# Opening products issued between the arms of a switch, tokens rounded to 16, scatters without order

## The chip, the cores and the metric

One core of a Trainium2 chip runs the whole program. The metric is device time in microseconds. Each kernel is run several times and the median is given; one execution is taken by the hardware profiler, and all rows and start times come from that one.

## The reference

Two stages. First, attention in chunks: 4 batches, 8 heads, 768 positions of 64 numbers; each chunk of 32 queries sees 8 memory keys, its own chunk, 16 keys to the left and 8 to the right. The outputs of all heads make a row x of 512 numbers for each of the 3072 tokens. Second, a mixture of 8 experts that drops no token:

```python
logits = x @ w_gate
expert_idx = np.argmax(logits, axis=1)
# gate_w: the softmax of the chosen expert
h = np.maximum(x_sorted[lo:hi] @ w1[e], 0.0)     # 512 -> 1024
y_sorted[lo:hi] = h @ w2[e]                       # 1024 -> 512
return gate_w[:, None] * y
```

All is fp32. How many tokens an expert has depends on the data. On the inputs of the reference the experts 0 to 7 get 529, 195, 426, 381, 565, 320, 162 and 494 tokens.

## The kernel before

**Attention and sorting** take the first 180 us or so. Finished rows of x are scattered by GpSimd into a DRAM area with one region for each expert. The first 256 tokens of expert 0 are worked on early, with plain matmuls (L1224, L1240). Meanwhile `count_up` counts the tokens of the experts, divides them into steps of STEP = 32 (rounded up) and writes `cases`, one number for each expert, and `good`, which says that the ordinary program's assumptions hold.

**The experts** come one after the other. Since the number of tokens is known only at run time, the program holds one copy of the body (an arm) for each possible number of steps: `tc.Switch(index[e], CASES)` with 33 arms. Each of the five engines loads the 8 numbers into registers (`loads`), and jumps on its own into the arm: in the trace these are COMPARE_BRANCH rows of line 1287, one for leaving an arm and one for entering the next.

**A body** (`expert`) of n tokens splits them into two halves of hf = n/2 columns, and computes both layers in a scheme of Strassen's kind: seven products of quarter matrices in the place of eight, and sums of quarters on VectorE. The first layer has 7 products for each of 2 column pairs, each of 4 matmuls; `product(i, bank, ...)` (L1081 is its matmul) writes one of six PSUM banks, taken in turn. The order on the engines is written out by hand (`manual_schedule`). A body opens with products 1 and 2 of both pairs into banks 0 to 3. ACT copies product 1 (L1107), VectorE adds product 2 (L1108). Then TensorE transposes two groups of the previous expert's result (`put_back`: `turn_y`, a scaling on ACT, and a scatter to `out` by GpSimd, L1021), goes on with product 6, transposes the other two groups, and so on. In the second half of the first layer it also transposes the next expert's tokens into `xT` (`turn_x`), and in `between` VectorE makes their sums and those of the next weights. The second layer has seven products of 8 matmuls, the last of them product 3 into bank 5, which `result` adds after the Switch (L1164).

More than 512 tokens are worked on in two bodies, one after the other, in one arm (expert 4); the argument `new` of `first_layer` is true in the first of them.

**Queues.** SyncE fetches the weights: four pieces of 512 KB for each layer, each behind the last reader of its buffer. GpSimd gathers the tokens of expert e + 2 in body e and scatters the results of expert e - 1. Since all scatters write the same tensor `out`, each of them waits until the one before has landed. After the last expert four more put-backs follow, then all engines load `good` (L1261) and jump over the general program, which runs when `good` is 0 (L1262).

Each fp32 matmul stands in the trace as two MATMUL rows with two LDWEIGHTS rows.

Of the kernel before, what the change touches and what calls it, by code (L numbers as in the profile page):

```python
# [70 lines left out]
XC = 1024  # L71
DX = 528
SKIP = 4096
STEP = 32
CASES = XC // STEP + 1
CAP = 512
HALF = CAP // 2
# [10 lines left out]
def parts(n):  # L88

    n1 = n if n <= CAP else STEP * -(-n // (2 * STEP))  # L90
    return [w for w in (n1, n - n1) if w]
# [419 lines left out]
def ordinary(ctx, tc, q, k, v, mem_k, mem_v, moe_w_gate, moe_w1, moe_w2, out, good):  # L511
# [503 lines left out]
    def gated(py, gate):  # L1015
        y = mpool.tile([128, DM], F32, name="y", bufs=4)
        nc.scalar.activation(y, py, AF.Copy, scale=gate)  # L1017
        return y

    def store(y, token):  # L1020
        nc.gpsimd.indirect_dma_start(  # L1021
            out=out,
            out_offset=bass.IndirectOffsetOnAxis(ap=token.bitcast(I32), axis=0),
            in_=y,
            in_offset=None,
            bounds_check=N - 1,
            oob_is_err=False,
        )

    def put_back(yT, tg, g):  # L1030

# [44 lines left out]
    def product(i, bank, w, a, q0):  # L1076

        hf, k = a[i].shape[2], a[i].shape[1]
        for q in range(2):
            for c in range(k):  # L1080
                mm(  # L1081
                    bank[:, q, 0:hf],
                    lhsT=w[i][:, c, 128 * (q0 + q) : 128 * (q0 + q) + 128],
                    rhs=a[i][:, c],
                    start=c == 0,
                    stop=c == k - 1,
                )
        return bank[:, :, 0:hf]

    def sums_of_x():  # L1090
        a = halves(xT, KX, HALF)
        sums(a, xS, slice(0, KX // 2))
        sum4(a, xS, slice(0, KX // 2))

    def first_layer(e, hf, backs, turns, new):

        a = halves(xT, KX, hf)
        w, a = weights(e, 0), streams(a, xS[:, :, :, 0:hf])
        hh, s = halves(h, KH, hf), hS[:, :, :, 0:hf]
        relu = lambda o: nc.scalar.activation(o, o, AF.Relu)  # L1100
        T = lambda i: tmp[:, i, :, 0:hf]
        C = lambda p: slice(2 * p, 2 * p + 2)
        to = lambda i, j, p: hh[i][j][:, C(p)]
        turn_of = iter(range(14))
        P = lambda i, p: product(i, banks[next(turn_of) % 6], w, a, 2 * p)
        for p in range(2):
            nc.scalar.copy(T(p), P(1, p))  # L1107
            i = add(to(0, 0, p), T(p), P(2, p), op=OP.add)  # L1108
            if p == 0 and new and e + 1 < E:
                for n in range(4):  # L1110
                    fetch_w(e + 1, 0, n, after=i)
            relu(to(0, 0, p))
        for f in backs[:2]:
            f()
        for p in range(2):
            add(T(p), T(p), P(6, p), op=OP.add)
        for f in backs[2:]:
            f()
        for p in range(2):
            add(T(2 + p), T(p), P(7, p), op=OP.add)  # L1120
        if new:
            sum_weights(e, 1, (5, 6))
        for p in range(2):
            p5 = P(5, p)
            add(to(1, 1, p), T(2 + p), p5, op=OP.add)  # L1125
            relu(to(1, 1, p))
            add(T(p), T(p), p5, op=OP.add)
        if new:
            sum_weights(e, 1, (4,))
        for p in range(2):  # L1130
            add(to(1, 0, p), T(2 + p), P(4, p), op=OP.add)
            relu(to(1, 0, p))
        for f in turns[:1]:
            f()
        for p in range(2):
            sums(hh, s, C(p))
            p3 = P(3, p)
            for f in turns[1:2] if p == 0 else turns[2:]:
                f()
            add(to(0, 1, p), T(p), p3, op=OP.add)  # L1140
            relu(to(0, 1, p))
        for p in range(2):
            sum4(hh, s, C(p))
        if new:
            sum_weights(e, 1, (7,))

    def second_layer(e, hf, yT, between):
        w, a = weights(e, 1), streams(halves(h, KH, hf), hS[:, :, :, 0:hf])
        p1, u2, u3 = (tmp[:, i, :, 0:hf] for i in (0, 4, 5))
        P = lambda i, b: product(i, banks[b], w, a, 0)  # L1150
        nc.scalar.copy(p1, P(1, 2))
        between()
        p4, p5 = P(4, 3), P(5, 4)
        add(u2, p1, P(6, 0), op=OP.add)
        add(u3, u2, P(7, 1), op=OP.add)
        add(yT[:, 2:4, 1, 0:hf], u3, p5, op=OP.add)
        add(u2, u2, p5, op=OP.add)
        add(yT[:, 0:2, 1, 0:hf], u3, p4, op=OP.add)
        add(yT[:, 0:2, 0, 0:hf], p1, P(2, 2), op=OP.add)
        P(3, 5)  # L1160

    def result(yT):
# [3 lines left out]
    def expert(e, n):  # L1166


        ps = parts(n)
        both = lambda f, *x: [lambda g=g: f(*x, g) for g in range(4)]  # L1170
        backs = both(put_back, yTs[(e - 1) % 2], tgs[(e - 1) % 2]) if e else []
        yT = yTs[e % 2]
        x = xes[e % 2]
        if len(ps) == 2:
            fetch_x(xe2, e, 1)
        for k, w in enumerate(ps or [0]):
            last = k + 1 >= len(ps)
            tg = tgs[e % 2 if last else 2]
            nc.vector.tensor_copy(tg, x[:, :, DM : DM + 2])
            if k == 0 and e + 2 < E:  # L1180
                fetch_x(x, e + 2, 0)
            x = xes[(e + 1) % 2] if last else xe2
            turns = both(turn_x, x) if not last or e + 1 < E else []
            if w:
                first_layer(e, w // 2, backs, turns, k == 0)
            else:
                for f in backs + turns:
                    f()
                if e + 1 < E:
                    for i in range(4):  # L1190
                        fetch_w(e + 1, 0, i)
            if last and e + 1 < E:
                for i in range(4):
                    fetch_w(e + 1, 1, i)

            def between():
                if turns:
                    sums_of_x()
                if last and e + 1 < E:
                    sum_weights(e + 1, 0)  # L1200

            if w:
                second_layer(e, w // 2, yT, between)
            else:
                between()
            if not last:
                result(yT)
                backs = both(put_back, yT, tg)

    def loads(engines, c, n):  # L1210
        return {eng.engine: eng.value_load(cases[0:1, c : c + 1], min_val=0, max_val=n - 1) for eng in engines}

    with tc.manual_schedule():
        choose(last)
        label(last)

        w1 = ws[0][0].rearrange("p (k n) -> p k n", n=F)
        w2 = ws[0][1].rearrange("p (k n) -> p k n", n=DM)
        for g in range(2):
            turn_x(xe2, g)  # L1220
        for f in range(KH):
            ph = banks[f % 4][:, 0]
            for c in range(KX):
                mm(ph, lhsT=w1[:, c, 128 * f : 128 * f + 128], rhs=xT[:, c, 0], start=c == 0, stop=c == KX - 1)  # L1224
            nc.scalar.activation(h[:, f, 0], ph, AF.Relu)
            if f == 1:
                rank(last, banks[4].rearrange("p a b -> p (a b)"))()
                count_up(banks[5])
                scatter(sent, NB)
        for t in [xes[1]] + yTs:  # L1230
            nc.vector.memset(t, 0.0)
        engines = (nc.tensor, nc.scalar, nc.vector, nc.gpsimd, nc.sync)
        index = [loads(engines, e, CASES) for e in range(E)]
        fetch_x(xes[0], 0, 0)
        fetch_x(xes[1], 1, 0)
        sum_weights(0, 0)
        for g in range(2):
            py = banks[4 + g].rearrange("p a b -> p (a b)")
            for f in range(KH):
                mm(py, lhsT=h[:, f, 0, 128 * g : 128 * g + 128], rhs=w2[:, f], start=f == 0, stop=f == KH - 1)  # L1240
            if g == 0:
                for g2 in range(4):
                    turn_x(xes[0], g2)
                sums_of_x()
            y = gated(py, xe2[:, g, DM + 1 : DM + 2])
            store(y, xe2[:, g, DM : DM + 1])
        for e in range(E):
            for a in tc.Switch(index[e], CASES):  # L1248
                expert(e, STEP * a)
            result(yTs[e % 2])  # L1250
        for g in range(4):
            put_back(yTs[(E - 1) % 2], tgs[(E - 1) % 2], g)


@with_exitstack
def kernel(ctx, tc, *args):
    nc = tc.nc
    gpool = ctx.enter_context(tc.tile_pool(name="gpool", bufs=1))
    good = gpool.tile([1, 1], I32, name="good")
    ordinary(tc, *args, good)  # L1260
    rv = nc.values_load(good[0:1, 0:1], min_val=0, max_val=1)  # L1261
    with tc.If(rv == 0):  # L1262
        general(tc, *args)

# [27 lines left out]
```

## Time and profile before

| | us |
|---|---|
| median of 6 runs | 607.2 (604.97 to 610.85) |
| profiled execution, its own time | 609.69 |
| its span, first to last instruction | 607.9 |
| TensorE busy in the span | 527.9 (87%) |
| mean granted clock of TensorE | 0.932 |
| experts' part, first opening to last product | 207.9 to 575.6 |
| idle before the openings of the bodies | 28.6 |

The widths hf seen in the trace are 144 (expert 0), 112, 224, 192, 144 twice (expert 4), 160, 96 and 256.

How to read it: a group's line has the source line, engine, operation, output and inputs, shapes and count, then the busy time and the mean of one in ns, then the idle time of the engine just before the group's instructions and what ended it. "issue" stands for a wait in which the profile shows nothing that was waited for. In timeline rows the first two numbers are start and duration. PEclk is the granted share of TensorE's clock in 40 slices of the span, in tenths.

### The profile page before, as it was taken

How to read it: one execution, taken by the hardware profiler on the slowest of the kernel's cores; microseconds unless marked ns; L12 is line 12 of the kernel's file. 1: busy time of each engine (PE TensorE's matmuls, PEld its weight loads, DVE VectorE, ACT ScalarE, POOL GpSimd, SP SyncE). 2: the span in 40 equal slices, each digit the busy share in tenths (PEclk: the TensorE clock that was granted, in tenths of full speed). 3: DMA queues.
4: the chain of work that ended last, by engine and by line, in shares of the span. 5: the costliest groups of instructions: out<-in, count | busy, mean ns of one | idle time of the engine just before them, and what ended most of it. 6: DMA issues, size and time to landing. Idle time of an engine off the chain costs nothing. (4 is left out here: it accounts for less than half of the span.)

```text
span 607.9 us, 10606 instructions
## 1 busy us (share of the span) xinstructions
PE 527.9 (87%) x3850; PEld 502.9 (83%) x3850; DVE 324.3 (53%) x757; ACT 176.2 (29%) x414; POOL 132.3 (22%) x174
## 2 busy tenths in 40 slices
PE   4999999999998998986998997999979799699900
PEld 3999899999976697986997997999879699588800
DVE  4556556565447286491782592655719639156300
ACT  3566365655311230221310320414023022122010
POOL 3500211412346320412200313301031011020020
PEclk9999899999869999997998998999979989799965
DMA  9999999997223190722520822503246063000010
GB/s 174 187 176 185 231 177 229 225 208 163 61 83 99 63 334 13 278 97 91 188 76 8 280 104 58 192 9 101 87 161 225 13 225 105 6 23 2 3 69 3
DMA packets 81658, 76.17 MB, mean 125 GB/s; under 512 B 39852, under 2 KB 64556, under 8 KB 81456
## 3 DMA queue, kind: packets, MB, share of 16 engines
q1 hardware_dynamic: 72368, 54.54, 38.2%
q0 software_dynamic: 8128, 19.29, 9.8%
q14 instruction: 147, 1.20, 0.7%
q8 instruction: 55, 0.90, 0.7%
q10 hardware_dynamic: 960, 0.24, 0.2%
HBM read 65.04 MB, written 16.45 MB: 134 GB/s over the span
## 5 line engine op out<-in xcount | busy, mean ns | idle before, releaser
L1081 PE MATMUL b<-xT,w 128*128 128x144 f32 (+6 forms) x288 | 58.4, 377 | 28.6 <-issue 25.6
L1081 PEld LDWEIGHTS b<-xT,w 128*128 128x128 f32 x288 | 54.6, 246 | 32.6 <-issue 30.6
L1021 POOL DMA_INDIRECT out_dram<-y,tg x36 | 38.1, 1058 | 199.7 <-ACT y L1017 101.1
L1100 ACT ACTIVATE h<-h 128x288 f32<-128x288 f32 (+6 forms) x72 | 33.7, 476 | 92.9 <-DVE h L1125 37.8
L686 PE MATMUL o<-v,ex 128*96 128x65 f32 x512 | 56.2, 255 | 0.9 <-PE o L686 0.9
L686 PEld LDWEIGHTS o<-v,ex 128*96 128x96 f32 x512 | 52.8, 171 | 1.1 <-issue 1.1
L1107 ACT COPY big<-b 128x288 f32<-128x288 f32 (+6 forms) x18 | 7.8, 431 | 152.9 <-PE b L1081 152.6
L662 PE MATMUL sc<-qT,kT 128*128 128x192 f32 x256 | 51.0, 345 | 0.0
L675 ACT ACTIVATE ex<-sc,cst 128x256 f32<-128x256 f32 x96 | 38.4, 471 | 32.4 <-PE sc L662 32.1
L1081 PE MATMUL b<-xS,w 128*128 128x144 f32 (+6 forms) x288 | 45.6, 307 | 0.0
L825 POOL DMA_INDIRECT xe<-x_dram,rows x38 | 40.0, 1052 | 25.0 <-PE b L1081 9.8
L1081 PE MATMUL b<-xS,wT 128*128 128x144 f32 (+6 forms) x288 | 44.4, 307 | 0.0
L1081 PE MATMUL b<-big,w 128*128 128x144 f32 (+6 forms) x288 | 44.4, 307 | 0.0
L1081 PE MATMUL b<-h,w 128*128 128x144 f32 (+6 forms) x288 | 44.3, 307 | 0.0
L662 PEld LDWEIGHTS sc<-qT,kT 128*128 128x128 f32 x256 | 43.9, 202 | 0.0
L1081 PE MATMUL b<-big,wT 128*128 128x144 f32 (+6 forms) x288 | 42.9, 307 | 0.0
L1081 PEld LDWEIGHTS b<-big,w 128*128 128x128 f32 x288 | 41.5, 190 | 0.8
L689 DVE RECIPROCAL inv_all<-o 96x4 f32<-96x4 f32 x64 | 11.4, 178 | 57.4 <-PE o L686 45.5
L1081 PEld LDWEIGHTS b<-h,w 128*128 128x128 f32 x288 | 41.3, 190 | 0.8
L1081 PEld LDWEIGHTS b<-xS,w 128*128 128x128 f32 x288 | 41.3, 191 | 0.8
L1081 PEld LDWEIGHTS b<-xS,wT 128*128 128x128 f32 x288 | 41.3, 190 | 0.8
L1081 PEld LDWEIGHTS b<-big,wT 128*128 128x128 f32 x288 | 41.0, 190 | 0.8
(150 smaller groups left out, 859.5 us busy)
## 6 DMA issues: line engine op xcount, KB each, us to landing
w<-in_moe_w_dram SPq DMA_DIRECT2D x64, 512.0 KB
kn<-in_k_dram SPq DMA_DIRECT2D x16, 384.0 KB
qn<-in_q_dram SPq DMA_DIRECT2D x16, 384.0 KB
v<-in_v_dram SPq DMA_DIRECT2D x24, 128.0 KB
v<-in_v_dram SPq DMA_DIRECT2D x24, 112.0 KB
v<-in_v_dram SPq DMA_DIRECT2D x8, 144.0 KB
v<-in_v_dram SPq DMA_DIRECT2D x8, 96.0 KB
xe<-x_dram,rows POOLq DMA_INDIRECT x38
```

The lines of the kernel that those rows point to most:

```text
L662: mm(sc[:, 2 * a : 2 * a + 2, 0:QB].rearrange("p x (j t) -> p x j t", j=2), lhsT=turned[b][:, a, w0 : w0 + WIN], rhs=units[i // 2]["qT"][: ...
L675: nc.scalar.activation(ex4[:, :, :, sl], sc4[:, :, :, sl], AF.Exp, bias=mask[:, 3 * x + g : 3 * x + g + 1], scale=D**-0.5)
L686: mm(o[:, j], lhsT=s["ex"][:, h], rhs=s["v"][:, h], start=True, stop=True)
L689: nc.vector.reciprocal(inv, o[:, :, D])
L825: nc.gpsimd.indirect_dma_start(out=to.bitcast(I32), out_offset=None, in_=x_dram, in_offset=bass.IndirectOffsetOnAxis(ap=which, axis=0), bo ...
L1021: nc.gpsimd.indirect_dma_start(out=out, out_offset=bass.IndirectOffsetOnAxis(ap=token.bitcast(I32), axis=0), in_=y, in_offset=None, bounds ...
L1081: mm(bank[:, q, 0:hf], lhsT=w[i][:, c, 128 * (q0 + q) : 128 * (q0 + q) + 128], rhs=a[i][:, c], start=c == 0, stop=c == k - 1,)
L1100: relu = lambda o: nc.scalar.activation(o, o, AF.Relu)
L1107: nc.scalar.copy(T(p), P(1, p))
```

## The change

The edits:
- STEP is 16, so there are 65 arms, and an expert's tokens are rounded up to 16.
- `lead(e)` issues products 1 and 2 of both pairs ahead of the Switch, in the full width of 256 columns, since the number of tokens is not known there. The first body in the arm takes the first hf columns of the banks and leaves these four products out.
- Scatters to `out` within one arm, or between two, are declared independent of each other (`stores`).
- For the last expert, the put-backs of groups 2 and 3 stand in the second layer ahead of its last product; groups 0 and 1 follow after the Switch.
- `good` is loaded into registers with the numbers of steps, ahead of the experts, and no longer at the end.

```diff
-STEP = 32
+STEP = 16
...
+    stores = []
+
     def store(y, token):
-        nc.gpsimd.indirect_dma_start(
+        i = nc.gpsimd.indirect_dma_start(
...
+        for j in stores:
+            tc.declare_no_dep(i.ins, j, reason="rows of different tokens")
+        stores.append(i.ins.name)
...
+    def lead(e):
+
+        a, w = streams(halves(xT, KX, HALF), xS), weights(e, 0)
+        for p in range(2):
+            product(1, banks[2 * p], w, a, 2 * p)
+            product(2, banks[2 * p + 1], w, a, 2 * p)
...
-        P = lambda i, p: product(i, banks[next(turn_of) % 6], w, a, 2 * p)
+
+        def P(i, p):
+            bank = banks[next(turn_of) % 6]
+            return bank[:, :, 0:hf] if new and i < 3 else product(i, bank, w, a, 2 * p)
...
         add(yT[:, 0:2, 0, 0:hf], p1, P(2, 2), op=OP.add)
+        if e + 1 == E and last:
+            for g in (2, 3):
+                put_back(yT, tgs[e % 2], g)
         P(3, 5)
...
         ps = parts(n)
+        del stores[:]
...
         index = [loads(engines, e, CASES) for e in range(E)]
+        in_range = nc.values_load(good[0:1, 0:1], min_val=0, max_val=1)
...
         for e in range(E):
+            lead(e)
             for a in tc.Switch(index[e], CASES):
                 expert(e, STEP * a)
+            del stores[:]
             result(yTs[e % 2])
-        for g in range(4):
+        for g in range(2):
             put_back(yTs[(E - 1) % 2], tgs[(E - 1) % 2], g)
+    return in_range
...
-    rv = nc.values_load(good[0:1, 0:1], min_val=0, max_val=1)
+    rv = ordinary(tc, *args, good)
```

More of the change, by code (lines that the diff above doesn't have):

```diff
@@ L1145, in first_layer, with second_layer @@
             sum_weights(e, 1, (7,))
-    def second_layer(e, hf, yT, between):
+    def second_layer(e, hf, yT, between, last):
         w, a = weights(e, 1), streams(halves(h, KH, hf), hS[:, :, :, 0:hf])
@@ L1202, in expert @@
             if w:
-                second_layer(e, w // 2, yT, between)
+                second_layer(e, w // 2, yT, between, last)
             else:
                 between()
+                if e + 1 == E:
+                    for g in (2, 3):
+                        put_back(yT, tg, g)
             if not last:
@@ L1259 @@
     good = gpool.tile([1, 1], I32, name="good")
-    ordinary(tc, *args, good)
-    rv = nc.values_load(good[0:1, 0:1], min_val=0, max_val=1)
+    rv = ordinary(tc, *args, good)
     with tc.If(rv == 0):
```

## The prediction

> **What bounds the kernel now.** I read the page first, then the experts' part (207 to 575 us) by shapes, then the timeline and the sequencer rows around one change of expert, then the tail.
>
> ```profile
> PE 527.9 (87%) x3850; PEld 502.9 (83%) x3850; DVE 324.3 (53%) x757; ACT 176.2 (29%) x414; POOL 132.3 (22%) x174
> PEclk9999899999869999997998998999979989799965
> L1081 PE MATMUL b<-xT,w 128*128 128x144 f32 (+6 forms) x288 | 58.4, 377 | 28.6 <-issue 25.6
> L1081 PE MATMUL b<-xS,w 128*128 128x144 f32 (+6 forms) x288 | 45.6, 307 | 0.0
> ```
>
> TensorE is busy for 87%, and no other engine for more than 53%. The two L1081 groups are equal numbers of equal shapes, yet the first, each body's products 1 and 2, costs 58.4 against 45.6 us and has 28.6 us of idle time before it. So the opening of each expert is dear. An fp32 matmul stands twice in the trace; I call one such row a piece. Four opening products are 32 pieces.
>
> ```profile
> L1081 PE MATMUL b<-xT,w 128*128 128x256 f32 x32 | 10.1, 490 | 5.1 <-issue 5.1
> L1081 PE MATMUL b<-xS,w 128*128 128x256 f32 x32 | 7.2, 379 | 0.0
> ...
> L1081 PE MATMUL b<-xS,w 128*128 128x112 f32 x32 | 4.0, 274 | 0.0
> L1081 PE MATMUL b<-xS,w 128*128 128x96 f32 x32 | 4.0, 272 | 0.0
> ```
>
> At 256 columns the opening takes 10.1 us, the same work later 7.2. At 112 and 96 columns 32 pieces cost the same 4.0 us: below some 128 columns a piece is held to 0.11 us. The starts in the timeline give 0.11 us a piece at 96 and 112 columns, 0.123 at 144, 0.136 at 160, 0.163 at 192, 0.189 at 224, 0.216 at 256.
>
> One change, expert 2 to 3: the timeline, two sequencer rows (last two figures: first and last start), and the windows' clock (after the busy time).
>
> ```profile
> 323.41 3.19 PE L1081 MATMUL b<-big,w 128*128 128x224 f32 x16
> 326.63 0.69 DVE L1164 TENSOR_TENSOR yT<-big,b 128x512 f32<-128x512 f32 x1 [2.40 <-PE b L1081]
> 329.40 7.12 PE L1081 MATMUL b<-xT,w 128*128 128x192 f32 x32 [2.81 <-issue]
> ```
> ```profile
> L1287 PEldq COMPARE_BRANCH  x2: 1091/2824/4558, 323.0 to 324.5; - x2
> ```
> ```profile
> 326.40:329.40 3.00, 0.20 (x2) 1.00 0.02 5
> ...
> 330.30:333.70 3.40, 3.40 (x12) 0.50 0.01 2
> ```
>
> TensorE's sequencer leaves the old arm at 323.05, 3.2 us before the last piece starts (326.24): 17 pieces of 0.189 us are queued. Leaving takes 1.09 us, the jump into the next arm 4.56, and the engine runs dry for 2.8. Then the granted clock is halved for 3.4 us. The same holds at all seven changes: the run-ahead is 16.8 to 17 pieces each time, the jump 4.44 to 4.82 us, the idle time 3.0 to 5.2, and 3.4 or 6.8 us at half clock follow. At Switch 0 the jump costs nothing:
>
> ```profile
> L1287 PEldq COMPARE_BRANCH  x1: 3473/3473/3473, 201.1 to 201.1; - x1
> ```
> ```profile
> 201.03 7.03 PE L1240 MATMUL b<-w,h 128*128 128x512 f32 x16
> ...
> 207.90 4.08 PE L1081 MATMUL b<-xT,w 128*128 128x144 f32 x32
> ```
>
> Sixteen long pieces, 7 us, were queued ahead of a 3.47 us jump, and the opening follows without a gap.
>
> The end is a chain of four scatters on GpSimd, each waiting for the landing of the one before:
>
> ```profile
> 577.82 0.98 POOL L1021 DMA_INDIRECT out_dram<-y,tg  x1 [32.56 <-ACT y L1017]
> 583.53 0.98 POOL L1021 DMA_INDIRECT out_dram<-y,tg  x1 [4.73 <-DMA out_dram<-y,tg]
> 587.07 0.98 POOL L1021 DMA_INDIRECT out_dram<-y,tg  x1 [2.55 <-DMA out_dram<-y,tg]
> 590.58 0.99 POOL L1021 DMA_INDIRECT out_dram<-y,tg  x1 [2.53 <-DMA out_dram<-y,tg]
> ```
>
> From the last issue to the end of the span (607.9) it is 17.3 us of landing, semaphores and an 8.9 us drain; the change does not touch these.
>
> **Part 1, lead(e).** The 32 opening pieces go in front of the Switch at full width 256, so the queue is full of them when the sequencer jumps. *Before*, from the start of the old expert's last piece to the first transposition of the new arm, the seven openings take 8.6, 13.4, 10.1, 9.5, 12.2, 10.8 and 15.3 us: 79.8. *After*, each is the old piece's slot (0.11 to 0.19, together 1.0), 32 x 0.216 = 6.9, and what of the jump stays open. The jump: 0.34 us from the last dispatch to the branch, 4.56, then 0.34 to the first weight load (all as at 324 to 329): 5.24. Cover: 16.8 x 0.216 + 0.22 = 3.84. Open: 1.4 us. Sum 1.0 + 7 x 8.3 = 59.2, a saving of 20.6. Leaving the old arm (0.3 to 2.2 us, and 0.35 of semaphore waits) is hidden by 16.8 old pieces, except after the 112- and 96-column experts: 0.8 back. **-19.8.** This takes the clock as whole: 1.4 us of idle time is at most 41% of a 3.41 us step of the clock record. Steps 55% and 59% busy (190.3 and 258.6 us) kept full clock; steps 32% busy or less lost it at all seven changes.
>
> [...]
>
> Waits of lead: its banks' last reader is VectorE's add from bank 2, done at 324.2, 2 us before the old arm's end; weights and xT were ready long before. Behind it on TensorE stands only the arm. The latest thing near is the result's add, done at 327.3, 0.7 us after the old arm's last piece: bounds 0 and 0.7 us a change. Nothing in the code asks for it, so I take 0. VectorE comes to the arm at 330.4 as before, while the lead runs to 333.5, so its 3 us jump lies under the lead.
>
> **Switch 0** had no gap, so it loses: 32 x (0.216 - 0.123) = 3.0, plus 0.34 + 3.47 + 0.34 - 3.84 = 0.3 open. **+3.3.**
>
> **Part 2, steps of 16.** The reference's routing, counted on its inputs, leaves 273, 195, 426, 381, 565, 320, 162, 494 tokens (expert 0 without the 256 done early). Only experts 1, 2, 6, 7 shrink, by 8 columns a half: 112 to 104, 224 to 216, 96 to 88, 256 to 248. Experts 1 and 6 lie on the 0.11 us floor: nothing. Experts 2 and 7 save 6.7 ns on each of the 192 pieces outside the lead: **-2.6**. Bounds 0 and -5.1. The doubled number of arms: today's jumps into arms 6 to 18 all take 4.4 to 4.8 us (3.47 into the first), so distance costs nothing visible. I take no change; the bounds are those rows, 1.1 us less and 0.3 us more a change.
>
> **Part 3, scatters.** The 46.0 us in which GpSimd waits for scatters inside the bodies are on nobody's path: from 207 to 576 us TensorE waits for the jumps and 3.0 us for ACT's copies, never for GpSimd. Worth nothing there. At the end the second half's two put-backs move ahead of product 3. Their yT is ready at 571.3 and TensorE reaches them at 571.9, so no wait, but product 3 is 16 x 0.109 = 1.75 us later. Scatters of groups 2 and 3 at about 574.0 and 575.3. GpSimd then leaves the arm, 5.0 us as at 544.3 to 549.25, ready near 580.5. The result is added by 578.0, group 0's y is ready at 579.9; scatters 0 and 1 at about 580.7 and 582.15 instead of 590.58. **-8.4.** Bounds: -9.7 if leaving were free, -3.8 if the four still waited for each other.
>
> **Part 4, good loaded early.** A ninth register load on TensorE before L1240: its eight start 0.7 us apart (186.0 to 191.1). **+0.7.** `good` is written at 184.1, so no wait. The loads at the end were hidden by the last scatter; nothing comes back.
>
> **Sum** -19.8 + 3.3 - 2.6 - 8.4 + 0.7 = -26.8 on the profiled execution, 609.69 us around a span of 607.9: 582.9. The median of the six runs is 2.5 us lower: 607.2 - 26.8 = **580.4 us**.
>
> **The rivals.**
> - *The clock halves all the same.* For: the step's threshold lies somewhere between 32% and 55% busy, and two gaps may share a step. Before, half clock cost 1.7 to 3.0 us an opening, 15.4 in all: 595.8.
> - *The queue holds more than the dispatch rows show.* 7 x 1.4 less: 570.6. Against: 16.8 at every change.
> - *The jump is not covered, and it gets slower.* The place is the jump after the lead. If the sequencer enters it only when the lead is done (a wait drawn at the join), 5.0 us stay open, 7 x 3.6 = 25.2 more, half clock 15.4, and 3.5 + 1.7 at Switch 0: 626. It decides from about 3.0 us open at each change: 7 x 1.6 + 15.4 eats the gain. Against it speaks Switch 0.
> - *The scatters still wait.* 580.4 + 4.6 = 585.0.
>
> **How the numbers follow.** Forecast with the scatter case 0.72, half clock 0.14, full queue 0.06, uncovered 0.06, a mixture that ends near no change 0.02. Half a per cent, 3 us, is what a measurement here can tell from nothing. Faster 0.92, same 0.02, slower 0.06. The range leaves out the uncovered case alone and takes in the floor's and the scatters' bounds: 571 to 597.
>
> **What would show it.** Right: 1 to 2 us idle before the first instruction of each arm, PEclk without dips after 207 us, 7.2 us for each opening at 256 columns, and the last scatter issued near 564 us (582.15 less the 18.4 of the other terms). Wrong: half clock at the changes (first rival); a matmul of lead waiting for VectorE or a DMA (third); 3 to 5 us between the last scatters (fourth). Shorter products of experts 1 and 6 would refute the floor.

## The result and the profile after

| | before | after |
|---|---|---|
| median, first comparison (46 and 20 runs) | 608.58 us | 580.61 us |
| ratio | | 0.9536 [0.9514, 0.9558] |
| median, a later comparison (c1_after, 11 and 6 runs) | 601.17 us | 564.36 us |
| ratio | | 0.9369 [0.932, 0.9417] |
| profiled execution (first comparison), its own time | 609.69 us | 576.35 us |
| its span; mean granted clock | 607.9 us; 0.932 | 574.5 us; 0.967 |

The change makes the kernel faster. The predicted 580.4 us lies on the first median. It will turn out that it lies there for a wrong reason: the saving in one term of the sum was 9 us too small, and the profile of that measurement holds losses of about the same size that no experiment could tie to a part of the change. The profile of the later comparison has hardly any of these losses.

The page of the kernel after: the engines, the clock's slices, and the two groups of equal products.

```profile
PE 527.2 (92%) x3850; PEld 497.8 (87%) x3850; DVE 322.1 (56%) x757; ACT 175.1 (30%) x414; POOL 134.2 (23%) x174
PEclk9999999999968999998999999999999999999995
L1086 PE MATMUL b<-xT,w 128*128 128x256 f32 (+1 forms) x288 | 60.7, 369 | 0.0
L1086 PE MATMUL b<-xS,w 128*128 128x144 f32 (+6 forms) x288 | 46.0, 309 | 0.0
```

The opening products (b<-xT,w) now cost 60.7 us, 2.3 more than before, since 256 of their 288 pieces are 256 columns wide. The 28.6 us of idle time before them is 0.0. After the attention PEclk dips once, in slice 19 (259 to 273 us), before the end; what stands there is told below.

The same change of expert as in the prediction, 2 to 3. First the timeline of the kernel after (TensorE's rows), then TensorE's two branches with first and last start at the end of the row, then two windows of TensorE (length, busy time, pieces, granted clock).

```profile
321.43 3.08 PE L1086 MATMUL b<-big,w 128*128 128x216 f32 x16
324.35 7.07 PE L1086 MATMUL b<-xT,w 128*128 128x256 f32 x32
331.45 0.74 PE L1012 MATMUL ty<-cst,yT 128*128 128x128 f32 x5
```
```profile
L1314 PEldq COMPARE_BRANCH  x2: 301/1912/3522, 321.1 to 327.7; - x2
```
```profile
324.70:331.50 6.80, 6.77 (x33) 1.00 0.16 23
331.50:334.90 3.40, 3.40 (x24) 1.00 1.03 411
```

The old arm's last pieces, the 32 pieces of the lead and the new arm's first transposition follow each other with next to no gap, and the clock stays whole. The branch out takes 0.30 us (1.09 before) and the branch in 3.52 us (4.56 before). From the last dispatch before the branch (327.4) to the first weight load of the arm (331.4) it is 4.0 us. The 32 pieces end at 324.35 + 32 x 0.216 = 331.26. So 0.1 to 0.2 us stays open where the prediction had 1.4.

The tail, GpSimd's timeline of the kernel after:

```profile
550.10 0.99 POOL L1023 DMA_INDIRECT out_dram<-y,tg  x1 [30.83 <-ACT y L1017]
552.04 0.98 POOL L1023 DMA_INDIRECT out_dram<-y,tg  x1 [0.96 <-POOLq L1274]
558.17 0.98 POOL L1023 DMA_INDIRECT out_dram<-y,tg  x1 [5.14 <-issue]
559.46 0.99 POOL L1023 DMA_INDIRECT out_dram<-y,tg  x1 [0.30 <-issue]
```

Two scatters are issued before GpSimd leaves the arm, two after; 5.1 us between the pairs is the leaving, and none waits for a landing.

### The profile page after: what moved, and what is told of

Read it like the earlier page. It is cut to its first block, busy times and chain, and to the rows that moved or that the text cites. A ratio compares the mean times of both kernels' runs of the same rounds, so it can differ in the third digit from the quotient of the medians.

```text
span 574.5 us, 10593 instructions
## 1 busy us (share of the span) xinstructions
PE 527.2 (92%) x3850; PEld 497.8 (87%) x3850; DVE 322.1 (56%) x757; ACT 175.1 (30%) x414; POOL 134.2 (23%) x174
## 5 line engine op out<-in xcount | busy, mean ns | idle before, releaser
L1113 ACT ACTIVATE h<-h 128x288 f32<-128x288 f32 (+6 forms) x72 | 33.3, 470 | 106.3 <-DVE h L1142 43.9
L1086 PE MATMUL b<-xT,w 128*128 128x256 f32 (+1 forms) x288 | 60.7, 369 | 0.0
L1086 PEld LDWEIGHTS b<-xT,w 128*128 128x128 f32 x288 | 52.3, 190 | 6.7 <-issue 0.5
L686 PE MATMUL o<-v,ex 128*96 128x65 f32 x512 | 54.2, 249 | 1.0 <-PE o L686 1.0
L686 PEld LDWEIGHTS o<-v,ex 128*96 128x96 f32 x512 | 50.6, 165 | 1.1 <-issue 1.1
L662 PE MATMUL sc<-qT,kT 128*128 128x192 f32 x256 | 49.1, 336 | 0.0
L825 POOL DMA_INDIRECT xe<-x_dram,rows x38 | 41.8, 1099 | 24.9 <-PE b L1086 8.3
L675 ACT ACTIVATE ex<-sc,cst 128x256 f32<-128x256 f32 x96 | 38.4, 471 | 29.7 <-PE sc L662 29.3
L662 PEld LDWEIGHTS sc<-qT,kT 128*128 128x128 f32 x256 | 42.0, 195 | 0.0
```

The lines of the kernel that those rows point to most:

```text
L662: mm(sc[:, 2 * a : 2 * a + 2, 0:QB].rearrange("p x (j t) -> p x j t", j=2), lhsT=turned[b][:, a, w0 : w0 + WIN], rhs=units[i // 2]["qT"][: ...
L675: nc.scalar.activation(ex4[:, :, :, sl], sc4[:, :, :, sl], AF.Exp, bias=mask[:, 3 * x + g : 3 * x + g + 1], scale=D**-0.5)
L686: mm(o[:, j], lhsT=s["ex"][:, h], rhs=s["v"][:, h], start=True, stop=True)
L825: nc.gpsimd.indirect_dma_start(out=to.bitcast(I32), out_offset=None, in_=x_dram, in_offset=bass.IndirectOffsetOnAxis(ap=which, axis=0), bo ...
L1086: mm(bank[:, q, 0:hf], lhsT=w[i][:, c, 128 * (q0 + q) : 128 * (q0 + q) + 128], rhs=a[i][:, c], start=c == 0, stop=c == k - 1,)
```

## The experiments

Each part of the change is named by its place in the prediction: the lead (part 1), steps of 16 (2), scatters and tail (3), `good` early (4). Ratios are to the kernel before on the same chip.

**Steps of 16 alone (a1_step16).** The kernel before with one line changed:

```diff
-STEP = 32
+STEP = 16
```

> The kernel before with steps of 16 and nothing else. The floor theory: experts 1 and 6 gain nothing, since a piece of 112 or 96 columns already takes 0.11 us; experts 2 and 7 gain 224 pieces x 6.7 ns each, 3.0 us in all, 0.995 of before. The rival, that every column counts: 6.0 us, 0.990. On the jumps: into the next arm they took 4.4 to 4.8 us before and 3.3 to 3.9 us after the change. If the straight code between leaving and jumping made them cheaper, they are 4.4 to 4.8 us here; if the new arms did, 3.3 to 3.9.

Measured: 598.83 against 600.72 us, 0.9971 [0.9944, 0.9997]. TensorE's 15 recorded branches and the opening products:

```profile
L1287 PEldq COMPARE_BRANCH  x15: 332/4422/5162, 196.0 to 511.8; - x15
```
```profile
L1081 PE MATMUL b<-xT,w 128*128 128x144 f32 (+6 forms) x288 | 57.9, 376 | 30.2 <-issue 30.2
```

The interval holds 0.995 and not 0.990. The branches into the arms still take 4.42 to 5.16 us (min/median/max mixes them with the branches out), those into the seven later arms 4.77 us on average against 4.57 before, and 30.2 us stand idle before the openings, against 28.6. So twice as many arms do not cheapen the jump, and make it dearer by some 0.2 us on average. In the profiles the seven openings take 80.8 us against 79.8; the expected 3.0 us of the two shorter experts, less this 1.0, are about the 1.9 us measured.

**The lead alone (a2_lead).** The kernel before with `lead(e)` ahead of the Switch and the reuse of its banks in `first_layer`; STEP is 32, the scatters keep their order, `good` is loaded at the end.

```diff
+            lead(e)
             for a in tc.Switch(index[e], CASES):
```

> The kernel before with lead alone, 33 arms, scatters in order. If straight code makes the jump cheaper, jumps of 3.3 to 3.9 us, openings of 7.0 to 7.7 us as after the change, 29 us saved there and 3 lost at Switch 0: 26 us less than before, 0.957. If the new arms make it cheaper, jumps of 4.4 to 4.8 us, 1.4 us open each: 16.5 us less, 0.973. The body of expert 1 was 5.9 us longer after the change, with stretches in which its products came late; if the scatters one behind the other did that, the body is 27 us long here; if lead did, about 33 us and the gain is 20 us.

Measured: 577.21 against 600.72 us, 0.9607 [0.9566, 0.9647].

```profile
PEclk9999999999959999999999999999999999999965
L1081 PE MATMUL b<-xT,w 128*128 128x256 f32 (+1 forms) x288 | 60.7, 369 | 0.0
```
```profile
L1299 PEldq COMPARE_BRANCH  x16: 310/1794/3931, 205.9 to 540.5; - x16
```

No branch of the Switch takes more than 3.93 us (those into the seven later arms 3.26 to 3.93) and every branch out takes 0.31 to 0.33. The clock has no dip between the attention and the tail. So the shorter jump comes with the lead and with nothing else in the change, and the lead alone brings 23.5 us, where the prediction's terms for it (-19.8 and +3.3) make 16.5.

**Scatters, tail and `good` alone (a3_tail).** The kernel before with parts 3 and 4; STEP 32, no lead.

```diff
+        for j in stores:
+            tc.declare_no_dep(i.ins, j, reason="rows of different tokens")
...
+        if e + 1 == E and last:
+            for g in (2, 3):
+                put_back(yT, tgs[e % 2], g)
...
+        in_range = nc.values_load(good[0:1, 0:1], min_val=0, max_val=1)
```

> The kernel before with independent scatters, the two put-backs ahead of the last product and good loaded early; no lead, steps of 32. The tail theory: 8.4 us less at the end and 0.7 more before the experts, 7.7 us, 0.987. If scatters one behind the other starve the body of expert 1, that body takes 33 us and not 27, and 2 us are left of the gain, 0.997. If the four last scatters still waited for each other, 3.1 us, 0.995.

Measured: 590.17 against 600.72 us, 0.9837 [0.979, 0.9885]: 9.8 us by that ratio (10.6 by the medians), with an interval that holds the predicted 7.7 us, 0.987, and neither of the two rivals' ratios. Its last scatters start at 566.6, 568.5, 574.6 and 575.9 us, in the same pattern as above. Its branches into arms take 4.26 to 4.61 us, as before: independent scatters do nothing for the openings.

The product of the three ratios is 0.9971 x 0.9607 x 0.9837 = 0.9423. The whole change had given 0.9536. Either the parts disturb each other, or the first comparison held something else.

**The lead with steps of 16 (b3_lead16).** a2_lead with STEP = 16, to see whether 65 arms and the lead disturb each other.

> Lead and steps of 16, nothing else changed: scatters in order, all four put-backs at the end. If steps of 16 and lead add up, 0.9607 x 0.9971 = 0.958. If the 65 arms with lead are what disturbs the bodies, 0.968, and 33 us for the body of expert 1.

Measured: 578.89 against 607.28 us, 0.9549 [0.9504, 0.9594]. The product of the parts, 0.9971 x 0.9607 = 0.9579, lies in the interval; 0.968 does not. They add up.

**The change with ordered scatters in the bodies (b2_ordered, and c3_ordered again beside the change).** The order of scatters is drawn again inside the bodies, and only the four of the tail stay independent.

```diff
+        def back(yT, tg, g):
+            del stores[:]
+            put_back(yT, tg, g)
+
-        backs = both(put_back, yTs[(e - 1) % 2], tgs[(e - 1) % 2]) if e else []
+        backs = both(back, yTs[(e - 1) % 2], tgs[(e - 1) % 2]) if e else []
```

> The kernel after, with the scatters inside the bodies waiting for each other as before, and only the last expert's own put-backs independent. If the scatters one behind the other disturb the bodies once lead has filled the gaps, this is about 1% faster than after, 0.943, with 27 us for the body of expert 1. If they do nothing, as the prediction said, the same as after within 0.3%.

Measured: 570.70 against 607.28 us, 0.9406 [0.9369, 0.9443]. It looked as if the order were a gain. The repeat of the change that belonged beside it (b1_after) gave no result, so both were run side by side later.

**The change itself again (c1_after), and c3_ordered.**

> The changed kernel once more, on the same chip as its two variants here. If the scatters one behind the other cost it 1% at random, 0.952 to 0.956 again, above the ordered variant by 1%, and stretches of late products in some body of its profile. If the difference was one of chips and days, 0.941 to 0.945, the same as the ordered variant, and no such stretch.

> The kernel with ordered scatters in the bodies once more, to stand beside the changed kernel: 0.941 as before. If scatters one behind the other cost something, the changed kernel is 1% slower than this; if not, the two are the same.

Measured on one chip: 564.36 us for the change, 0.9369 [0.932, 0.9417]; 564.61 for the ordered one, 0.9386 [0.934, 0.9432]. There the order in the bodies is worth nothing, as the prediction had it. The change came out a little below both expected ratios; the 0.9423 of its parts lies just above its interval, and has itself an uncertainty of about 0.007 from the three intervals, so the two agree. The clock of c1_after has no dip between the attention and the tail (no half clock from 171 to 546 us).

What the first comparison lost shows, in part, in its profile. The timeline of the kernel after, in the body of expert 1 (weight loads of a product, later a transposition):

```profile
252.89 0.91 PEld L1086 LDWEIGHTS b<-xT,wT 128*128 128x128 f32 x7
254.32 0.52 PEld L1086 LDWEIGHTS b<-xT,wT 128*128 128x128 f32 x4 [0.53 <-issue]
255.78 0.52 PEld L1086 LDWEIGHTS b<-xT,wT 128*128 128x128 f32 x4 [0.94 <-issue]
...
263.76 1.81 PE L1006 MATMUL tx<-cst,xe 128*128 128x128 f32 x8 [1.97 <-ACT xT L1007]
```

The same product in c1_after, TensorE's timeline, is one group without a gap:

```profile
249.41 1.95 PE L1086 MATMUL b<-xT,wT 128*128 128x104 f32 x16
```

In the first, the 16 pieces come in groups of 7, 4, 4 and 1, with waits of 0.5 to 0.9 us between them in which the profile shows nothing that was waited for (the third wait ends at 257.2); half clock follows at 257.1 and 264.0 us, 3.4 us each, and the transpositions wait for ACT's copies. From the first transposition of the arm to the last piece ahead of the second layer's last two products that body took 29.3 us, and 21.8 in c1_after. By the same measure it took 23.4 us before, 22.0 in a2_lead, 21.9 in a3_tail, 23.4 in b2_ordered and 23.5 in b3_lead16; the 27 and 33 us of the expectations include 3.6 us for the last two products. No other profile shows this product in groups (a wait of about 2 us for ACT's copies alone stands at the same place before and in b2_ordered, b3_lead16 and b4_quarter_lead). c1_after has the same scatters and b3_lead16 the same 65 arms without such waits, so neither causes them each time, and no packet of the instruction queue 8 starts there (none between 248.9 and 265.8 us). That the unordered scatters cause them now and then is not excluded: four of them are issued at 251.1 to 255.1 us, beside the late product, and in the first comparison no ordered version ran beside the change. What the pieces waited for stays open.

**Half of the lead (a4_half_lead), and the same with ordered scatters (c2_half_ordered).** If the jump is 3.3 to 3.9 us and no longer 4.6, fewer pieces cover it. Only the first pair's two products are issued ahead; the second pair's go back into the arm, in the width of the expert.

```diff
-        for p in range(2):
+        for p in range(1):
...
-            return bank[:, :, 0:hf] if new and i < 3 else product(i, bank, w, a, 2 * p)
+            return bank[:, :, 0:hf] if new and i < 3 and p == 0 else product(i, bank, w, a, 2 * p)
```

> The kernel after with half a lead: products 1 and 2 of the first pair ahead of the Switch at 256 columns, those of the second pair in the arm at the arm's width. If the queue of some 17 pieces sets the cover, 16 pieces of 0.216 us cover as much as 32 do, the openings stay without a gap of over 1 us, and half of the added columns goes: 9 us less than after, about 571 us. If the cover goes by the length of the lead, some 2 to 3 us stay open at each Switch and the clock halves behind them: 580 to 590 us.

> Half a lead and ordered scatters in the bodies. The half lead alone gave 0.9293. If scatters one behind the other cost 1%, 0.920; if nothing, 0.929 again. Openings of 5.9 to 7.8 us, no half clock after 207 us.

Measured: 556.97 us, 0.9293 [0.9261, 0.9324] for the first; 555.98 us, 0.9262 [0.9215, 0.9309] for the second, beside c1_after's 564.36. The page of a4_half_lead:

```profile
PEclk9999999999969999999999999999999999999995
L1086 PE MATMUL b<-xT,w 128*128 128x256 f32 (+7 forms) x288 | 53.2, 339 | 2.6 <-issue 2.5
```

7.5 us of piece time goes (60.7 to 53.2) and 2.6 us of idle time comes, in gaps of 0.1 to 0.6 us; the clock stays whole from 168 to 536 us. The branches in still take 3.38 to 3.93 us. c2_half_ordered is the fastest version of this study, 8.4 us below the change on the same chip.

**A quarter of the lead (b4_quarter_lead).** Only product 1 of the first pair is ahead: 8 pieces of 0.216 us.

```diff
-            product(2, banks[2 * p + 1], w, a, 2 * p)
...
-            return bank[:, :, 0:hf] if new and i < 3 else product(i, bank, w, a, 2 * p)
+            return bank[:, :, 0:hf] if new and i == 1 and p == 0 else product(i, bank, w, a, 2 * p)
```

(with `range(1)` as above)

> The kernel after, with only product 1 of the first pair ahead of the Switch, 8 pieces. If the queue of some 17 pieces sets the cover, 8 wide pieces and the last 9 of the old expert cover 2.9 us of a jump of 3.6 and its 0.5 us of handling: about 1.1 us open at each change where the half lead has 0.5, 4.5 us more, against 4.5 us of columns saved: the same as the half lead, 0.93. If the jump costs 4.5 us again because it follows too soon on leaving the arm, 6 us more, or 12 with half clocks: 0.94 to 0.95.

Measured: 578.82 us, 0.9519 [0.9478, 0.956], just above the second expectation's 0.94 to 0.95. Its opening products, then TensorE's branches at two changes, expert 0 to 1 and 3 to 4:

```profile
PEclk9999999999958999999999899799998999999995
L1086 PE MATMUL b<-xT,w 128*128 128x144 f32 (+7 forms) x288 | 54.9, 352 | 15.8 <-issue 12.8
```
```profile
L1313 PEldq COMPARE_BRANCH  x2: 321/2348/4374, 236.0 to 237.3; - x2
```
```profile
L1313 PEldq COMPARE_BRANCH  x2: 315/1862/3409, 361.4 to 365.5; - x2
```

This kernel holds both kinds of jump. Where the branch in starts 1.2 to 1.4 us after the start of the branch out (0 to 1, 1 to 2, 5 to 6, 6 to 7) it takes 4.37, 4.24, 4.14 and 4.40 us. Where it starts 3.5 to 4.1 us after it (2 to 3, 3 to 4, 4 to 5), because the sequencer first stood still in the straight code (at 3 to 4 from 362.8 to 365.4 us), it takes 3.26, 3.41 and 3.57. So within one kernel and one run the jump is long where it follows the join closely, and short where it doesn't.

## Why the prediction was right or wrong, step by step

**The openings, predicted -19.8, measured -29.0: the mis-sized term.** From the old expert's last piece to the first transposition the seven openings take 7.37, 7.07, 7.28, 7.26, 7.03, 7.67 and 7.05 us, together 50.7 and not 59.2. The step that was mis-sized is "The jump: 0.34 us from the last dispatch to the branch, 4.56, then 0.34 to the first weight load (all as at 324 to 329): 5.24". It carried over the length of a jump from rows in which the jump stood right behind the join. With straight code between, the jumps take 3.25 to 3.85 us. The branches out, 0.3 to 2.2 us before, take 0.30 to 0.32, so the 0.8 us "back" is not there either. At most 0.6 us stays open where 1.4 was expected, seven times. The cover was sized right: at 327.4 us there were 3.9 us of pieces in hand, against 3.84. With the measured jump the same step gives 0.34 + 3.25 to 3.85 + 0.34, or 3.9 to 4.5 us, against 3.84: next to nothing open, as the deeper-queue rival had it for another reason.

A row that hinted at it was in the prediction: the branch at Switch 0, 3.47 us, the only one that does not follow a join. It was taken as a sign that distance costs nothing, not as a sign that the others are dear.

**Why the jump is shorter.** The page lists a DMA queue 8 of the kind "instruction" (before: 55 packets, 0.90 MB, so 16 KB each); before and after, one or two of its packets start within each of TensorE's branches into an arm. Change 2 to 3 before: the branch in starts at 324.5 us; a packet starts at 324.86 (1.54 us) and a second at 325.45, which takes 2.09 us; the jump ends at 329.0. After: one packet at 322.1 (0.96 us), long done when the branch in starts at 327.7; its packet starts at 328.64 and takes 1.20 us; the jump ends at 331.2. The last packet comes 0.97 us behind the branch in both, and it is 0.9 us longer in the first, of 1.04 us by which the jump is longer. b4_quarter_lead shows the same pair of cases: 237.62 and 238.25 us (2.03 us long) with the jump of 4.37 us; 362.91 and 366.48 (1.05 us) with that of 3.41.

It holds for all 96 branches into an arm in the twelve profiles. The last packet that starts within the branch lands 1.2 to 2.4 us before the branch ends, 1.4 in the median. In the 27 branches of 4.14 to 5.16 us another packet starts 0.4 to 1.2 us ahead of that one, which then takes 1.45 to 2.50 us. In the 69 branches of 3.25 to 3.95 us the one ahead starts 1.6 us or more earlier, and the last takes 0.88 to 1.53 us. So the rows of a long jump differ from those of a short one in the packet close ahead and in the longer last one. What code the two packets carry, and whether the first delays the second, is not shown. An overlap of the two is not needed: at change 3 to 4 before, the first has landed (371.4 us) when the second starts (371.5), which still takes 1.64 us. Why it does is not shown.

The branches out became short in all arms of kernels with a lead; without one only the first and the last expert's are. The packets fit that too: each of the six long ones before (1.09 to 2.16 us) has a packet that starts 0.25 to 1.26 us ahead of it, and ends 1.3 to 1.5 us after that packet has landed. In the kernels with a lead no packet stands there, and the page counts six fewer, 49 after against 55 before. That the long branches out wait for that packet would fit these rows, but is not shown; why there is none with the arms that have four products fewer was not tested.

**The clock, predicted whole: right.** No change of expert is followed by half clock in the change or in a2_lead. The openings' idle time of at most 0.6 us did not try the stated bound of 1.4 us; b4_quarter_lead did, with 1.6 to 3.4 us. The record of its clock goes in steps of 3.41 us; these windows lie on such steps (length, busy time, pieces, granted clock), in pairs of one with a gap and the one after it:

```profile
474.20:477.60 3.40, 2.12 (x11) 1.00 0.05 10
477.60:481.00 3.40, 3.07 (x28) 1.00 0.02 7
...
255.80:259.20 3.40, 1.60 (x15) 1.00 0.83 253
259.20:262.60 3.40, 3.40 (x19) 0.50 0.59 213
...
320.60:324.00 3.40, 1.18 (x7) 1.00 0.04 10
324.00:327.40 3.40, 3.40 (x11) 0.51 0.03 7
```

62% busy kept the clock; 47% and 35% lost it. In the experts' part of the twelve profiles no step at whole clock that was more than 52% busy was followed by half clock. So 1.4 us idle in 3.41, 59% busy, would most likely have been harmless there, as the prediction said. (On the steps it named, the profile's windows read 57% and 63% busy, where it said 55% and 59%, and one that lost the clock, at 272.2 us, reads 38% and not 32% or less.)

**Switch 0, predicted +3.3, measured +3.0**: its opening takes 6.96 us (205.18 to 212.14) against 3.92. The widening is all of it; no gap stands there, where 0.3 us was held to be open. Its branch took 3.36 us.

**Steps of 16, predicted -2.6, measured -2.4.** Expert 2's pieces save 1.3 us in all, expert 7's 1.1. By shapes, c1_after between 201 and 545 us (where expert 2 has 216 columns, 1 has 104 and 6 has 88):

```profile
L1086 PE MATMUL b<-xS,w 128*128 128x216 f32 x32 | 6.3, 346 | 0.0
...
L1086 PE MATMUL b<-xS,w 128*128 128x104 f32 x32 | 4.0, 273 | 0.0
L1086 PE MATMUL b<-xS,w 128*128 128x88 f32 x32 | 4.0, 272 | 0.0
```

104 and 88 columns cost the 4.0 us that 112 and 96 did. The floor holds at these four widths; no product of these runs is between 112 and 144 columns wide, so the "some 128 columns" below which the prediction has it are an estimate.

**Scatters and tail, predicted -8.4, measured -7.8**: from the last piece ahead of the second layer's last two products to the last scatter's issue it is 14.6 us after and 22.3 before. Leaving the arm took GpSimd 5.1 us, where 5.0 was taken over from the trace. Inside the bodies the order is worth nothing (c1_after against c3_ordered, on one chip). The last scatter is at 559.5 us, earlier than "near 564", by the openings.

**`good` early, predicted +0.7, measured +0.4** (TensorE's idle time ahead of the early products of the second layer grew from 1.72 to 2.07 us); it lies inside the start below.

**The sum.** On the profiled executions: openings -29.0, Switch 0 +3.0, steps -2.4, tail -7.8 make -36.2. Beside them, and not of the change: the first opening starts 2.7 us earlier (205.2 against 207.9; 198.8 to 207.9 over all profiles); last scatter to end of span 15.0 against 17.3 us (15.0 to 17.1 in kernels with either order); and 7.7 us more in the bodies, 5.9 of them in expert 1's. Together -33.5, and the times differ by 33.3. The median of the first comparison gains only 28.0: most of its runs were longer than the profiled one, at lower clocks (0.967 in the profiled run, mostly 0.958 to 0.964 in the others); where they lost time is not shown. The later comparison, whose profile has no late products, gains 36.8 us.

So the forecast's case was right in kind and in sign, four of its five terms within 0.6 us. The fifth was 9 us too small, and losses of some 8 us, which no experiment tied to a part of the change, brought the first median onto the forecast. That it lies within 0.2 us of it is luck. The range of 571 to 597 us holds that median; 0.9369 of 607.2, the later ratio on the time the prediction started from, is 568.9 and lies just below it.

Of the signs named for being right, the 1 to 2 us of idle time did not come (0.6 at most), and the clock did dip after 207 us, though inside a body and not at a change. Of the rivals, the uncovered jump and the scatters that still wait are refuted by the rows above; the halved clock is seen at no change. The deeper queue gave 570.6, near what the later comparison makes of it, but not by its mechanism: the pieces in hand were as many as predicted (3.9 us of them, against 3.84).

## What to carry to other kernels

Here a branch into an arm had a price of its own, 3.25 to 3.95 us, and a second one, 4.14 to 5.16 us in all, when it stood right behind the join of the arm before: put work whose operands are ready between the two, and measure the branch again with it before sizing the cover. Then trim the cover: half of the work ahead of the Switch hid the jump nearly as well and, in the right width, cost 8.4 us less. When a predicted number is met, check the terms one by one, and measure again beside the variants; here two errors of 8 to 9 us cancelled.

## What the runs showed that was not expected

- The length of TensorE's branch into an arm depends on what precedes it: 4.14 to 5.16 us when the sequencer comes to it within 1.1 us of the end of the branch out, 3.25 to 3.93 us when 1.7 us or more lie between. Into the first Switch, which follows no join, it took 3.36 to 3.95 us with a lead, but 3.47, 4.66 and 4.26 us in three kernels without. The packets fit that spread: in the second and third of these another starts 0.4 and 1.2 us ahead of the jump's own, in the first none within 6 us.
- The border at which the granted clock halved is not one busy share. In the experts' part it halved after a 3.4 us step that was 47% busy (255.8 us in b4_quarter_lead) and after one 52% busy (253.7 us in the kernel after), and stayed whole after one that was 46% busy (238.7 us in b4_quarter_lead). In the attention, whose matmuls are smaller, it halved after a step 72% busy (158.2 us in the kernel after, 2.45 of 3.40 us).
- One product of expert 1 came in four groups, with waits of 0.5 to 0.9 us between, in one profile of the change and not in its second profile; the profile names no cause.
